# Another order of all engines in the middle of an attention and mixer kernel

## The chip, the core and the metric

The kernel runs on one core of a Trainium2 chip. The core has five engines that each run their own instructions in order and wait for one another through semaphores: PE (TensorE, matmuls; its weight loads are listed as PEld), DVE (VectorE), ACT (ScalarE), POOL (GpSimd) and SP (SyncE). DMAs are issued by POOL (loads here), SP (stores and transposes) and, at the end, ACT. The metric is the device time of one execution in microseconds (us). The profile is of one execution; its span runs from the first to the last instruction.

## What is computed

Block-causal attention over 8 batches, 8 heads, 576 positions and 64 channels a head, and then a token- and channel-mixing MLP on the result, in float32 at both ends:

```python
scores = (1 / sqrt(D)) * q @ k.T                # (8, 8, 576, 576), allowed where i // 64 >= j // 64
attn = softmax(scores); x = heads_to_channels(attn @ v)    # (8, 576, 512)
u = x + (relu(x.T @ w_tok1) @ w_tok2).T                    # 576 -> 256 -> 576 tokens
out = u + relu(u @ w_ch1) @ w_ch2                          # 512 -> 1536 -> 512 channels
```

## The kernel before

The kernel first records all its work as 1526 numbered pieces (`P.add`), each with the engines that may run it, the pieces it depends on and the PSUM banks that it takes and gives back. Nothing in it is looped on the chip. The order is a table, `ORDER`, of 1514 entries: `placed` walks through it, and each entry emits its piece at that point on the engine that it names. An entry such as `367Tdebf` is piece 367 on T (PE) in the PSUM banks d, e, b and f; A is ACT, D is DVE, P is POOL and S is SP; a to d are the `mm` banks, e to h the `late` banks. So the table sets three things: the order on each engine, the engine of a piece that two can run, and the bank. What it does not set are the waits: a piece waits for its inputs and for its bank wherever it stands.

The pieces of one batch, with their lines before the change (after it every line below the table is 3 higher):

- loads on POOL: q and k into `qk_sb` (L417, four a batch: two head groups of four heads), V into `vals` (L469, five a batch); they convert to bf16
- L440 on DVE: transposes of q and k inside 32 x 32 blocks, two for each load
- L562 on PE: score sets, three for each head group, in 32 rows of the array for each of four heads at a time
- L777 on ACT: exponentials from four PSUM banks into `e_sb`; L588 a copy of a part of it and L599 zeros for barred keys, on POOL or DVE
- L616 on PE: attention times V for one head (128 x 128 array), L669 the last 64 positions of four heads (64 columns); L636, L642 and L691, L697 on DVE: reciprocals and scaled results into `x_sb`, which give the bank back
- L814, L818 token matmuls up, L913, L944, L953 down, L928 their sum on DVE; L980 and L990 on SP: DMA transposes of it from batch 2 on
- L1041, L1114, L1238 channel matmuls up, the latter two with seven products for eight; L393, L395, L800, L802 evacuate banks on ACT or DVE, L1153, L1271 join on DVE
- L1354 sums for the channel matmuls down on DVE, L1372 those matmuls (256 columns each), L1396 folds their banks into `o_sb`, L1438 on SP stores it (L1483 for batch 0)

Attention of later batches stands between the channel matmuls of earlier ones, so PE has both kinds of work to hand. The first 44 us hold the loads of the weights and batch 0; attention ends with batch 7 at about 173 us; after that only token and channel matmuls are left.

Of the kernel before, what the change touches and what calls it, by code (L numbers as in the profile page):

```python
# [27 lines left out]
class Plan:  # L28
# [69 lines left out]
    9D 8D 14S 7D 0A 15A 11S 41Ta 19P 69Tb 17P 1D 52Tb 21P 31P 25P 51Tb 65Tb 23P 29P 12A 27P 3D 2D 16D 20D 18D 22D  # L98
    13D 26D 24D 105Ts 106A 98Ttbc 61Td 57Td 49Td 99A 100D 30D 63Td 118A 122Ts 70Td 123A 78Td 62Td 54Td 102Tt 103A
    45Td 28D 104D 35P 34P 50Td 33P 158Ts 159A 142Tt 143A 32P 74Td 181P 178P 101D 55Td 115Td 68Tb 125Ts 107Tb 184P  # L100
    108T 116D 117D 124D 183D 119A 162Tt 182D 160D 47Td 179D 40P 126A 138Ts 59Td 37P 42Td 109D 111Td 112T 120D 121D
    163A 66Tc 180D 145Tt 110D 39P 113D 144D 38P 36P 139A 135Tc 136D 114D 79P 127Ta 128T 131Tb 132T 133D 165Ts 80P
    140D 82P 161P 53Td 141D 146A 60Td 147Td 137D 129D 130D 166A 151Tc 152T 148T 134D 46Ta 44Ta 202Tabef 206A 204A
    205A 164D 185D 175Tg 153D 154D 155Th 149D 176D 177D 156D 157D 267Tc 268D 150D 203A 265Tg 167Th 208Tcbfe 266A
    187P 168T 81P 88P 87P 84P 83P 171Tg 89P 210A 269Td 209A 270A 90P 172T 211A 86P 85P 212A 343P 188D 273Tb 189D
    169D 170D 186D 277Th 173D 241Tdcaf 245A 174D 271Tg 10P 274D 244A 242A 275Tb 281Tf 278D 279Th 272D 285Tg 280A
    276D 195Tbdae 198A 197A 4D 282D 5D 286D 283Th 284D 310Tf 319Tg 287Th 288A 316Td 295Ta 317T 318D 320T 196A 243A
    322Th 323T 321A 199A 228Tdcbg 324A 200D 289Te 207D 290T 232A 230A 261D 296T 297A 6D 345D 311T 312D 231A 191P
    229A 192P 301Tc 193P 262D 346P 302T 235Taghb 239A 291A 236A 292Td 293T 233D 190P 194P 201P 344D 304Tb 294D 305T
    348D 234D 298Te 299T 347D 352P 216Td 219Ta 220D 237A 303A 217D 218D 213Tc 222Tg 306A 214D 223D 300A 238A 215D  # L110
    240D 225Th 226D 224D 367Tdebf 370A 227D 221D 313Tc 314T 369A 255Th 315D 373Tagbe 246Tc 368A 353D 371A 375A 354D
    307Td 376A 349P 247D 377A 256D 91P 248D 252Tf 308T 309A 257D 350D 351D 374A 258Tb 253D 360Tcegh 362A 361A 259D
    522P 364A 254D 334Td 249Te 519P 250D 251D 338Tf 393Thcae 260D 428Tb 395A 263D 264D 363A 520D 523D 396A 429D 397A
    394A 398D 426Tc 427A 92P 339T 372P 406Theag 409A 408A 93P 358P 432Tc 524D 433D 434Tb 435D 407A 340T 341D
    400Tceah 410A 430Tg 431D 436Tf 437D 335T 442Tg 404A 444Th 445D 403A 357P 521D 355P 402A 365P 359P 366P 401A
    446Tf 356P 378Tc 379D 387Te 388D 381Th 384Ta 405P 382D 389D 390Tb 447A 443A 380D 528P 391D 383D 392D 438Tg 385D
    399P 423Tc 424D 439A 536Thefb 537A 538A 539A 440Tg 540A 386D 336T 417Ta 425D 325Tc 549Tbfeh 94D 95D 441A 551A
    96D 450D 552A 531P 525P 97D 337D 329Tg 330T 454Tef 532P 553A 685P 451D 550A 533P 418D 535P 331T 411Tb 529D 332D
    527D 412D 413D 326T 420Tg 688P 421D 414Td 457A 460T 461A 469Thb 419D 422D 472A 455Ta 526D 691P 456A 415D 416D
    530D 470Tg 471A 541D 542P 327T 475T 476A 458Tg 452D 328D 453D 473Ta 543Tdhce 700P 459A 462T 687D 464T 474A 479T  # L120
    477T 546A 463D 547A 534P 544A 545A 690D 478D 569Tdgec 573A 572A 571A 701P 689D 480D 602Th 570A 603D 604Tc 605A
    576Thgea 578A 580A 548P 566Td 482T 577A 465D 466D 574D 467T 468A 694P 567D 568D 686D 612Td 613D 483D 582Thagc
    579A 585A 606Tf 857P 586A 557Te 610Td 581D 481D 584A 484Tbg 485Tc 611D 615S 583A 558D 487A 560Ta 559D 448Th 449A
    607D 608Td 486A 561D 609D 614S 490T 488Tf 491A 562D 554Th 692D 489A 563Te 564D 709Tabdc 711A 555D 556D 494T 342S
    565D 495D 492T 493D 575P 593Te 594D 590Th 591D 587Tb 588D 592D 710A 713A 712A 714P 497T 595D 498D 715Tdfca 333S
    589D 854P 599Th 596Te 597D 496A 697P 699P 695D 598D 716A 600D 719A 601D 870P 718A 696D 499D 500D 503Tgd 717A
    501D 504A 702Tebca 704A 616D 620Tfh 698P 623A 706A 863P 505T 693D 860P 705A 703A 707D 626T 627A 635Tab 507Tc
    638A 502D 641T 642A 506D 509T 508D 748Tgafe 751A 511T 617D 510D 512D 749A 859D 618D 858D 954P 752A 750A 513T
    735Tcaeg 736A 739A 708D 867P 770Tf 619D 514D 771A 855D 636Tc 737A 637D 856D 738A 740P 639Tg 515T 516D 742Tecaf
    862D 640A 645T 646D 745A 726Td 727D 643T 644D 865D 746A 720Ta 868P 768Tf 648T 723Tg 769D 721D 744A 728D 724D  # L130
    725D 624Tc 778Tf 722D 779D 774Td 729Tg 730D 731D 625A 628T 649A 776Ta 743A 747P 621Te 622A 777D 780Tg 781A 775D
    732Ta 783S 871Tdefb 874A 873A 875A 733D 629D 772Tg 647D 734D 741P 753Tc 773D 630T 650Tfa 653A 872A 762Tg 631D
    651Tb 652A 861D 759Te 754D 633T 755D 763D 764D 656T 657D 760D 761D 654Tb 634A 655A 878Tgchd 880A 879A 881A 864D
    765Tf 766D 660T 767D 756Te 757D 661D 658T 782S 819Tgf 758D 882A 822A 517S 804Thc 964P 807A 663T 659D 785D 786D
    789Tde 664A 792A 825T 632D 790Tb 787D 826A 662D 665D 951P 965P 960P 808Ta 809A 791A 866P 795T 796D 805Tg 810T
    806A 812T 813D 811A 793Tb 794A 814T 815D 917Thdga 799T 788D 876P 800D 797T 798D 918A 666D 919A 920A 921A 869P
    957P 820Th 817T 818A 823Tg 824A 802T 803A 967P 884Tabdc 888A 886A 821D 885A 887A 883P 667D 829T 827T 669Teh 670A
    830D 832T 956D 833A 828D 953D 904Tdabc 907A 877P 901Tg 668D 906A 902D 905A 955D 903D 908A 963P 952D 1051P 671T
    672D 911Tdabf 912A 914A 961D 895Tg 896D 897D 898Tc 899D 892Te 893D 915A 913A 900D 894D 937Td 938A 889Tg 981Tcafb
    985A 916D 909P 910P 890D 931Te 958D 932D 933D 984A 982A 673Td 891D 934Tg 983A 816A 959D 1057P 968Tecfb 970A 935D  # L140
    966P 936D 674D 972A 922Ta 923D 1054P 971A 924D 925Tg 926D 962D 1060P 927D 969A 675T 676D 928Ta 1066P 929D
    1008Tgfbc 1010A 677T 1011A 973P 1012A 1009A 930D 678D 975Tabfe 977A 979A 1053D 683S 679T 978A 1014Tebdg 1052D
    976A 680D 1015A 1017A 1055D 1016A 831D 939Tf 940D 1001Teacd 1018A 1002A 1004A 1062D 980P 974P 992Tb 986Tf 1003A
    1063P 995Tg 1061D 1056D 989Te 990D 1005A 993D 994D 1065P 991D 996D 681T 998Td 987D 1068Tebac 1071A 997D 1070A
    1072A 999D 988D 1069A 682D 943Tg 1000D 1036Tf 1058D 801D 1075Tdbha 1077A 1076A 944D 1006P 1079A 1059D 1037A
# [1441 lines left out]
```

## Time and profile before

| what | us |
|---|---|
| device time, median of 3 runs | 284.17 (284.06 to 284.25) |
| profiled execution, span of the core | 282.2 |
| what lies around the span, by the median | 2.0 |
| PE busy | 275.3 |
| DVE busy | 238.8 |
| ACT busy | 177.8 |
| POOL busy | 78.8 |
| last matmul ends, about | 278.7 |
| median landing of a 128 KB V load on POOL's queue | 5.9 |
| median landing of a 288 KB q load on POOL's queue | 6.1 |
| median landing of a 512 KB store on SP's queue | 3.0 |

Busy time on PE runs to the modelled end of each matmul, so back-to-back matmuls overlap in it and a busy PE may still be held back by a little less than one matmul's length; the step from start to start is the better measure. Sizes of the loads are those written, in bf16. A name such as `late<-vals,e_sb` says what an instruction writes and reads; PEclk, the granted clock, is full speed in all slices of the span.

### The profile page before, as it was taken

The page shows a single profiled execution, that of the slowest core. Times are in us where ns is not written, and L with a number is a line of the kernel's source. Part 1 is how long each engine was busy: PE and PEld are TensorE (multiplying, and loading weights), DVE is VectorE, ACT ScalarE, POOL GpSimd, SP SyncE. Part 2 cuts the span into 40 slices and gives each one's busy share as a digit, 9 for nine tenths or more (in the row PEclk, how much of TensorE's full clock was granted, in tenths as well). Part 3 has the DMA queues.
Part 4 walks back from the last instruction along what each step waited for, and adds up shares of the span by engine and source line. Part 5 has one row for each costly group of instructions (what it writes and reads, how often), then busy time and mean ns, then how long its engine had stood idle before and what let it go on. Part 6 is the DMA issues. An engine that isn't in the chain of part 4 may idle for free.

```text
span 282.2 us, 8544 instructions
## 1 busy us (share of the span) xinstructions
PE 275.3 (98%) x3580; PEld 193.2 (68%) x3580; DVE 238.8 (85%) x523; ACT 177.8 (63%) x326; POOL 78.8 (28%) x131
## 2 busy tenths in 40 slices
PE   7899999999999999999999999999999999999994
PEld 2457665475768877888776658744589664788884
DVE  4589598889889989999988879887797898898974
ACT  4788888775899774899997990326840858530000
POOL 8876726371613422092257210000000000000000
PEclk9999999999999999999999999999999999999999
DMA  8999999959958947699399465150127200020555
GB/s 160 167 153 194 191 200 203 162 63 170 95 88 229 150 67 56 151 104 127 46 118 161 31 141 120 42 114 19 37 49 210 80 0 0 3 75 14 212 126 174
DMA packets 64918, 31.75 MB, mean 112 GB/s; under 512 B 53104, under 2 KB 56176, under 8 KB 64880
## 3 DMA queue, kind: packets, MB, share of 16 engines
q0 software_dynamic: 45040, 17.64, 54.0%
q1 hardware_dynamic: 19408, 12.91, 16.7%
q10 hardware_dynamic: 432, 0.66, 0.7%
q8 instruction: 28, 0.46, 0.7%
q14 instruction: 10, 0.08, 0.1%
HBM read 35.85 MB, written 9.44 MB: 160 GB/s over the span
## 4 chain that ended last, share of the span: by engine, by line
PE 82%; DMA 10%; DVE 3%; ACT 2%; POOL 1%; issue 1%; DVEq 0%; POOLq 0%
PE mm L1372 13%; PE late L1372 11%; DMA qk_sb<-in_q_dram 7%; PE late L1114 7%; PE late L1238 6%; PE mm L1114 6%; PE mm L1238 6%; PE mm L562 4%; PE late L616 3%; DMA wc_sb<-in_moe_w_ch_dram 3%; PE late L562 3%; PE late L913 3%; PE mm L814 2%; PE mm L616 2%; PE late L814 2%; PE mm L913 2%
## 5 line engine op out<-in xcount | busy, mean ns | idle before, releaser
L777 ACT ACTIVATE e_sb<-mm 128x512 bf16<-128x512 f32 x94 | 53.5, 612 | 9.8 <-PE mm L562 4.2
L777 ACT ACTIVATE e_sb<-late 128x512 bf16<-128x512 f32 x74 | 43.0, 613 | 5.6 <-PE late L562 2.7
L440 DVE STREAM_TRANSPOSE qk_sb<-qk_sb 128x288 int32<-128x288 int32 (+2 forms) x57 | 38.3, 695 | 6.0 <-ACT qk_sb L393 1.9
L469 POOL DMA_DIRECT2D vals<-in_v_dram x45 | 37.1, 833 | 8.5 <-PE late L616 7.5
L1372 PEld LDWEIGHTS <-sums 128*128 128x128 bf16 x288 | 27.8, 98 | 4.2 <-issue 0.4
L1372 PEld LDWEIGHTS <-gT 128*128 128x128 bf16 x288 | 27.9, 98 | 3.7
L562 PEld LDWEIGHTS <-qk_sb 32*64 32x64 bf16 (+1 forms) x1024 | 16.9, 99 | 16.5 <-issue 9.6
L562 PE MATMUL mm<-qk_sb 32*64 32x320 bf16 (+6 forms) x534 | 27.7, 273 | 0.0
L616 PEld LDWEIGHTS <-e_sb 128*128 128x128 bf16 x640 | 23.9, 97 | 5.4 <-issue 0.9
L393 ACT COPY late<-mm 128x512 f32<-128x512 f32 (+1 forms) x14 | 8.0, 571 | 27.6 <-DVE o_sb L1396 14.5
L562 PE MATMUL late<-qk_sb 32*64 32x320 bf16 (+6 forms) x382 | 25.0, 277 | 0.3 <-DVE x_sb L642 0.3
L1114 PEld LDWEIGHTS <-ws_sb 128*128 128x128 bf16 x192 | 17.9, 98 | 4.2 <-issue 0.9
L599 POOL MEMSET e_sb<- 64x512 bf16 (+1 forms) x23 | 11.4, 511 | 31.7 <-ACT e_sb L777 28.4
L800 ACT ACTIVATE gT<-late 128x512 bf16<-128x512 f32 x20 | 12.2, 611 | 7.4 <-PE late L1114 4.9
L1114 PEld LDWEIGHTS <-wc_sb 128*128 128x128 bf16 x144 | 15.5, 113 | 1.8
L1238 PEld LDWEIGHTS <-ws_sb 128*128 128x128 bf16 x96 | 9.4, 98 | 9.8
L616 PE MATMUL late<-vals,e_sb 128*128 128x65 bf16 x360 | 15.8, 193 | 0.0
L642 DVE TENSOR_TENSOR x_sb<-late,rinv 128x256 bf16<-128x256 f32 x36 | 14.8, 418 | 0.7
L580 ACT ACTIVATE e_sb<-sc 128x1024 bf16<-128x1024 f32 x11 | 10.8, 1026 | 4.5 <-PE sc L562 4.5
L1372 PE MATMUL mm<-wd_sb,sums 128*128 128x256 bf16 x108 | 13.1, 273 | 0.0
L616 PE MATMUL mm<-vals,e_sb 128*128 128x65 bf16 x280 | 12.4, 193 | 0.0
L417 POOL DMA_DIRECT2D qk_sb<-in_k_dram x12 | 6.6, 551 | 20.7 <-ACT e_sb L777 7.1
(203 smaller groups left out, 649.4 us busy)
## 6 DMA issues: line engine op xcount, KB each, us to landing
out_dram<-o_sb SPq DMA_DIRECT2D x14, 512.0 KB, 3.0
vals<-in_v_dram POOLq DMA_DIRECT2D x28, 128.0 KB, 5.9
qk_sb<-in_k_dram POOLq DMA_DIRECT2D x12, 288.0 KB, 5.6
qk_sb<-in_q_dram POOLq DMA_DIRECT2D x12, 288.0 KB, 6.1
wc_sb<-in_moe_w_ch_dram POOLq DMA_DIRECT2D x8, 192.0 KB, 7.8
wc_sb<-in_moe_w_ch_dram POOLq DMA_DIRECT2D x3, 512.0 KB, 8.0
out_dram<-o_sb SPq DMA_DIRECT2D x4, 256.0 KB, 3.2
vals<-in_v_dram POOLq DMA_DIRECT2D x15, 64.0 KB, 5.4
```

The lines of the kernel that those rows point to most:

```text
L440: nc.vector.transpose(dst[:, 0:S, :] .rearrange("p s e -> p (s e)") .bitcast(I32) .rearrange("p (a k) -> p k a", k=NB)[:, k0:k1], raw2.bit ...
L469: nc.gpsimd.dma_start(out=t[128 - p : 128, J, hs, 0:64], in_=src)
L562: nc.tensor.matmul(out=home(n)[rows, c : c + w], lhsT=kT[i][r, 64 * j : 64 * j + keys, par], rhs=qT[i][r, 64 * q : 64 * q + w, par], start ...
L599: (nc.vector if o.engine == "DVE" else nc.gpsimd).memset(late_keys, 0.0)
L616: nc.tensor.matmul(out=u[:, I, 0:65], lhsT=e[:, h, c : c + 128], rhs=vt[:, J, head, 0:65], start=(J == 0), stop=(J == I),)
L642: nc.vector.tensor_tensor(out=xt[:, 0:4, 64 * head : 64 * head + 64], in0=u[:, :, 0:64], in1=ri[:, 0:4].to_broadcast([128, 4, 64]), op=MULT,)
L777: nc.scalar.activation(dst, bank_of(x), EXP, scale=scale)
L800: nc.scalar.activation(dst, src, RELU)
L913: nc.tensor.matmul(out=bank_of(bank), lhsT=w2_sb[:, t, 128 * si : 128 * si + 128], rhs=at[:, t, :], start=(t == 0), stop=(t == NDT - 1),)
L1114: nc.tensor.matmul(out=bank_of(bank)[:, 256 * o_ : 256 * o_ + 256], lhsT=x(o_, m), rhs=y[:, :, m, :], start=opens, stop=m == 1, skip_group ...
L1238: nc.tensor.matmul(out=bank_of(bank), lhsT=x(m), rhs=y[:, :, m, :], start=first and m == 0, stop=m == 1, skip_group_check=not first,)
L1372: nc.tensor.matmul(out=bank_of(bank)[:, 256 * i : 256 * i + 256], lhsT=x[:, kk, 128 * i : 128 * i + 128], rhs=y[:, kk], start=first and i ...
```

## The change

Only `ORDER` differs. All 1514 entries are there in both, the first 288 are the same, and the last 72 name the same pieces on the same engines, five of them with another bank letter. Between them the order of all engines is another one; 73 pieces change their engine (33 from ACT to DVE, 32 from DVE to ACT, 6 from DVE to POOL, 2 from POOL to DVE), and many banks change. The change is described as one that keeps loads away from stores. One line of each, the first that differs:

```diff
-    240D 225Th 226D 224D 367Tdebf 370A 227D 221D 313Tc 314T 369A 255Th 315D 373Tagbe 246Tc 368A 353D 371A 375A 354D
...
+    213Tc 222Tg 306A 214D 223D 300A 238A 215D 240D 225Th 226D 224D 367Tfbde 349P 91P 258Tc 369A 227D 92P 221D
```

The first place is on POOL, some 140 us into the run, where q and k of batch 7 are loaded. Before, its rows are these; the two q loads in one row are those of head groups 0 and 1 of batch 7, and the k loads ahead of them are the ones that go with them:

```order
L417 DMA qk_sb<-in_k_dram 128x1152
L588 COPY vals<-e_sb 128x256
L599 MEMSET e_sb 64x4x2x64
L417 DMA qk_sb<-in_k_dram 128x1152
L469 DMA vals<-in_v_dram 128x8x64
L417 DMA qk_sb<-in_q_dram 128x1152 x2
L469 DMA vals<-in_v_dram 128x8x64
L588 COPY vals<-e_sb 128x256
L599 MEMSET e_sb 64x4x2x64 x2
L469 DMA vals<-in_v_dram 128x8x64 x2
```

After, the same four loads, the q of head group 0 first, stand like this:

```order
L420 DMA qk_sb<-in_q_dram 128x1152
L591 COPY vals<-e_sb 128x256
L602 MEMSET e_sb 64x4x2x64
L420 DMA qk_sb<-in_k_dram 128x1152
L602 MEMSET e_sb 64x4x2x64
L420 DMA qk_sb<-in_q_dram 128x1152
L591 COPY vals<-e_sb 128x256
L602 MEMSET e_sb 64x4x2x64
L472 DMA vals<-in_v_dram 64x8x64
L420 DMA qk_sb<-in_k_dram 128x1152
L472 DMA vals<-in_v_dram 128x8x64 x2
```

The q load of head group 1 was issued last of the four, right behind the other q load; now it is issued third, with a copy, memsets and the k load of its group around it.

The second place is on DVE and belongs to the first: the transposes of those loads among the results of attention in batch 6 (L642). Before, the row of three transposes holds both of the q load of head group 1 and the second one of the other q load:

```order
L440 STREAM_TRANSPOSE qk_sb<-qk_sb 128x9x32
L1168 TENSOR_SCALAR gT<-gT 128x4x256
L802 TENSOR_SCALAR aT<-late 128x512
L440 STREAM_TRANSPOSE qk_sb<-qk_sb 128x9x32 x3
L636 RECIPROCAL rinv<-late 128x4
L636 RECIPROCAL rinv<-mm 128x4
L642 TENSOR_TENSOR x_sb<-mm,rinv 128x4x64
L642 TENSOR_TENSOR x_sb<-late,rinv 128x4x64
```

After, the last row is the first transpose of the q load of head group 1:

```order
L443 STREAM_TRANSPOSE qk_sb<-qk_sb 128x9x32
L639 RECIPROCAL rinv<-late 128x4
L639 RECIPROCAL rinv<-mm 128x4
L645 TENSOR_TENSOR x_sb<-mm,rinv 128x4x64
L645 TENSOR_TENSOR x_sb<-late,rinv 128x4x64
L639 RECIPROCAL rinv<-mm 128x4
L645 TENSOR_TENSOR x_sb<-mm,rinv 128x4x64
L645 TENSOR_TENSOR x_sb<-late,rinv 128x4x64
L443 STREAM_TRANSPOSE qk_sb<-qk_sb 128x9x32
```

Four results and their reciprocals have moved ahead of the transposes that read that q load.

The third place is on POOL again, where V of batch 4 is loaded. Before, the V row of two and the last V row are three of its five loads, with a V half of batch 5 between them:

```order
L599 MEMSET e_sb 64x4x2x64 x2
L417 DMA qk_sb<-in_k_dram 128x1152
L469 DMA vals<-in_v_dram 128x8x64 x2
L469 DMA vals<-in_v_dram 64x8x64
L469 DMA vals<-in_v_dram 128x8x64
L417 DMA qk_sb<-in_q_dram 128x1152
L417 DMA qk_sb<-in_k_dram 128x1152
```

After, the same row of two is the only one here of batch 4; the V rows on either side are of batch 5:

```order
L420 DMA qk_sb<-in_q_dram 128x1152 x2
L591 COPY vals<-e_sb 128x256
L602 MEMSET e_sb 64x4x2x64
L472 DMA vals<-in_v_dram 128x8x64
L420 DMA qk_sb<-in_k_dram 128x1152
L602 MEMSET e_sb 64x4x2x64
L472 DMA vals<-in_v_dram 128x8x64 x2
L472 DMA vals<-in_v_dram 64x8x64
L472 DMA vals<-in_v_dram 128x8x64
```

The two loads have moved behind two q loads, another V load, a k load and a copy with its memset; in the table they now stand directly ahead of the first L619 (L616 before) of batch 4. On SP the first store L1441 (L1438 before) has moved ahead of the second pair of transposes L983 (L980 before).

More of the change, by code (lines that the diff above doesn't have):

```diff
@@ new lines @@
+    543Tbghe 423Ta 547A 530D 546A 700P 687D 464T 690D 424D 698P 462T 463D 545A 544A 548P 473Te 474A 425D 694P
+    465D 438Th 439A 569Tacbg 479T 570A 554Th 573A 571A 477T 480D 478D 557Ta 558D 555D 556D 686D 691P 467T 572A
+    559D 482T 574D 468D 466A 576Tbceg 577A 483A 481D 602Th 578A 560Ta 561D 604Tb 579A 580A 562D 603A 605D
+    582Tacdf 583A 484Teg 487A 581D 585A 689D 608Tb 854P 609D 448Th 612Ta 613D 490T 575P 584A 563Tb 606Td 491A
+    701P 564D 610Ta 565D 488Tc 449A 586A 611D 607D 489A 566Th 567D 568D 709Tafbe 713A 485Td 693D 494T 486D 495D
@@ new lines @@
+    710A 492T 493D 712A 711A 599Ta 600D 715Tdheb 716A 497T 498A 614S 496D 596Tf 718A 601D 719A 717A 597D 598D
+    593Tc 587Td 588D 589D 503Tga 504A 594D 595D 615S 616D 590Tf 869P 702Tcdbe 706A 591D 592D 505T 620Tef 499D
+    704A 703A 623A 617D 635Tdh 636Tc 638A 637A 692D 506D 696D 507Tg 857P 770Tc 705A 641T 626T 500D 771A 333S
+    695D 501D 627D 342S 509T 508D 856D 642A 748Tdebc 511T 752A 502D 863P 621Tc 749A 707P 510D 751A 512D 750A
+    618D 639Td 640D 619D 513T 858D 514D 622A 735Tbceg 737A 736A 708P 738A 868P 859D 643T 644D 860P 645T 855D
@@ new lines @@
+    515T 516D 739A 646D 624Tc 647D 625A 742Tdebg 745A 714P 743A 697P 699P 723Ta 724D 870P 867P 628T 629D 740P
+    744A 630T 741P 631D 648T 746A 729Tb 720Tc 747P 725D 726Td 727D 730D 721D 731D 722D 768Te 649A 517S 756Ta
+    732Tc 728D 871Tbdgh 769A 772Te 873A 874A 872A 757D 758D 733D 734D 862D 773D 778Tc 779D 776Td 633T 650Tea
+    774Tc 777D 775D 759Tg 760D 761D 861D 753Tb 754D 762Td 783S 763D 954P 634A 653A 654Tf 656T 764D 655A 755D
+    632D 651Tc 657A 652A 660T 658T 659D 875A 876P 661D 878Tbced 877P 765Tg 964P 881A 879A 782S 882A 766D 780Tf
@@ new lines @@
+    890D 912A 898Tf 937Th 938A 903D 891D 892Tb 968Tacde 972A 969A 1051P 899D 916P 900D 893D 962D 970A 894D 1060P
+    675T 981Tebaf 971A 973P 958D 974P 934Tc 667D 668D 982A 967P 935D 931Td 932D 959D 928Th 922Te 929D 923D 924D
+    985A 936D 930D 673Tf 674D 984A 925Te 1057P 926D 927D 983A 1008Tbach 1010A 1012A 933D 1011A 677T 1009A
+    975Tdeah 965P 676D 977A 678D 831D 978A 979A 1063P 679T 1053D 1056D 1001Tbace 976A 1004A 680D 980D 1003A
+    1002A 939Tf 1005A 1052D 940D 1055D 1014Tadch 998Tb 1017A 992Tf 801A 1018A 995Te 999D 1000D 986Tc 989Tb 993D
@@ new lines @@
+    1058D 1006P 518S 681T 996D 1013P 990D 1015A 991D 997D 987D 988D 1007P 941Ta 994D 1016A 1068Tecdb 1031Th
+    1069A 1062D 1072A 1071A 945Tf 682D 942D 1064P 1065P 1025Te 1026D 1070A 946D 1027D 1036Tg 1037A 1075Tadbf
+    1028Tc 1076A 1061D 1059D 1032D 943Te 1033D 1022Tg 1023D 1077A 1078A 1034Ta 1079A 1035A 1066P 944D 1024D
+    1019Tb 1020D 1021D 1067P 1029D 1030D 816D 1108Tdehg 1112A 1110A 1109A 1046Tf 1047D 683S 1050S 1101Tabcg
+    1080D 1105A 1103A 1038Te 1039D 947Td 948D 950S 1044Tg 1073P 1111A 1268Tf 1113P 1104A 1102A 834D 1045D
@@ new lines @@
+    1149D 1151T 1296S 852S 1281S 1274Th 1212A 1414D 1207D 1145A 1147D 1417Tbe 1275D 1280S 1418Ta 1152A 1205A
+    1228D 1432Tdg 1290Th 1291D 1419A 1229D 1230D 1232Tcf 1433Ta 1415D 1420A 1233A 1231D 1423T 1234T 1235D 1225D
+    1238T 1239D 1236Tc 1242T 1297S 1237D 1243D 1240T 1299D 1300D 1421Th 1435A 1244T 1241D 1245D 1301D 1434A
+    1422A 1363Tac 1438T 1425T 1364Tf 1424A 1366A 1180A 1416D 1365A 1427T 1367Tb 1369T 1426D 1439A 1348Tfh 1428D
+    1430T 1368A 1351A 1371T 1165D 1302D 1431A 1372D 1349Td 1350A 1354T 1352Te 1373T 1374D 1436Td 1437D 1355A
```

125 lines of the change are left out of this document (49 added, 76 removed).

## The prediction

> **What bounds the kernel now.** I read the page first, then the busy times by stretch, then the list of who waited for whom on PE (TensorE), and at last the chain of waits. The page says that PE is hardly ever idle:
>
> ```profile
> span 282.2 us, 8544 instructions
> PE 275.3 (98%) x3580; PEld 193.2 (68%) x3580; DVE 238.8 (85%) x523; ACT 177.8 (63%) x326; POOL 78.8 (28%) x131
> ```
>
> A share over the whole span doesn't say where the rest lies. The view by stretch does (columns: length, then busy time and instructions of PE, PEld, DVE, ACT, POOL). I cut it at 44 us, where the first moved piece of PE's work starts, and at about 259 us, where the common end begins:
>
> ```profile
> 0.00:23.00 23.00, 20.14 (x290) 10.34 (x291) 14.46 (x50) 15.35 (x20) 18.94 (x36) 1.00 1.21 163
> 23.00:44.00 21.00, 20.78 (x352) 13.92 (x349) 17.34 (x45) 17.83 (x37) 10.85 (x19) 1.00 1.37 196
> 44.00:150.00 106.00, 106.00 (x1698) 76.64 (x1702) 96.90 (x224) 86.51 (x168) 42.03 (x65) 1.00 0.95 121
> 150.00:156.00 6.00, 5.69 (x160) 4.46 (x144) 5.46 (x17) 3.92 (x9) 4.64 (x7) 1.00 1.12 136
> 156.00:259.00 103.00, 103.00 (x926) 70.57 (x923) 88.46 (x160) 53.87 (x97) 2.36 (x5) 1.00 0.27 63
> ```
>
> PE is idle for 2.86 us before 23 us and 0.22 us up to 44 us; both lie in the part of the order that stays. In the 215 us whose order changes it is idle for 0.31 us, all of it between 150 and 156 us. The granted clock is 1.00 throughout. The waits of PE name the pieces:
>
> ```profile
> PE late L562 <- DVE x_sb L642: 0.3, 1, 0.3
> PE late L669 <- ACT e_sb L777: 0.2, 1, 0.2
> PE mm L814 <- DVE x_sb L642: 0.2, 1, 0.2
> ```
>
> The second is the 0.22 us before 44 us, the third belongs to the first 23 us. Only the first can go.
>
> Busy isn't yet full speed, since a matmul's record is longer than its step. So I look at the step, in the chain of waits, whose pieces run from one start to the next:
>
> ```profile
> 203.72 0.86 PE mm L1238 x4
> 255.67 2.62 PE mm L1372 x24
> ```
>
> A matmul of 512 columns takes 0.86 / 4 = 0.215 us and one of 256 columns 2.62 / 24 = 0.109 us: twice the columns, twice the time, so these pieces are bound by the columns streamed and nothing waits in them. The Trainium skill (TensorE: Matmul & The Clock Gate, Back-to-back issue gap) gives about 131 ns a matmul for a sustained stream at 512 columns, and N/2.4 + 2.5 ns for the isolated gap. By the first the long matmuls would have 39% of room and an order could win microseconds; the rows give 215 ns, which is the second, so the measurement decides and there is no such room.
>
> **The change, part by part.** Both programs hold the same matmuls (3580), in another sequence between 44 and about 259 us. So PE's own sum is the same, and only three things on it can change: its waits, its switches between array shapes, and nothing at the ends, which both orders share (the 2.0 us between the span of 282.2 and the median of 284.17 stays as well: I forecast changes against the profiled span and add them to the median).
>
> *The wait at 153.97 us.* The chain and PE's timeline show it:
>
> ```profile
> 143.94 7.26 DMA qk_sb<-in_q_dram
> ...
> 151.30 0.68 DVE qk_sb L440
> ...
> 152.40 0.70 DVE qk_sb L440
> ...
> 153.16 0.77 DVE x_sb L642 x2
> ...
> 153.97 0.30 PE late L562
> ```
>
> ```profile
> 153.46 0.20 PE L669 MATMUL mm<-vals 128*64 128x65 bf16 x2
> 153.97 0.30 PE L562 MATMUL late<-qk_sb 32*64 32x320 bf16 x1 [0.31 <-DVE x_sb L642]
> ```
>
> POOL issues a q load of batch 7 at 143.94 us, it lands 7.26 us later, DVE stands at its transposes until then, and only afterwards empties the PSUM banks of batch 6 (L642) that the scores of batch 7 need. The two short matmuls from 153.46 us step 65 columns each, some 0.06 us together, and a switch takes 0.10 (below), so L562 could have started at 153.62: the wait costs 0.35 us. In the new order DVE's rows have four L645 (L642 before) and their reciprocals ahead of the transpose pair of that load, and on POOL the load stands ahead of a V half, a k load and two V loads, where it followed a k, a V and the other q load. Both take this wait away. What is late next on PE there is unknown; the neighbouring stretches have no idle time, so I take minus 0.35 us.
>
> *Switches of shape.* L562 uses 32 rows of the array, L669, L944 and L953 use 64 columns, all else 128 by 128. PE's timeline around one set of scores shows the price:
>
> ```profile
> 97.09 1.47 PE L1372 MATMUL mm<-wd_sb,sums 128*128 128x256 bf16 x12
> 98.50 0.39 PE L562 MATMUL late<-qk_sb 32*128 32x512 bf16 x1
> ...
> 98.75 0.38 PE L562 MATMUL late<-qk_sb 32*128 32x512 bf16 x2
> 99.06 1.16 PE L1372 MATMUL mm<-wc_sb,sums 128*128 128x256 bf16 x9
> ```
>
> Twelve steps of 0.109 end at 98.40, and L562 starts at 98.50; its last 512 columns, from 98.75, end at 98.96, and L1372 starts at 99.06: 0.10 us a switch, each way. Counted over PE's whole order there are 121 switches before and 123 now, because sets of scores border less often on other work in small shapes: plus 2 x 0.10 = 0.20 us.
>
> *Work that changes engine.* 33 evacuations and casts go from ACT to DVE and 32 the other way, 6 small copies and memsets from DVE to POOL and 2 back. DVE (96.90 of 106 us busy in the long stretch) keeps about its load: one evacuation more, four small ones less. I take nothing; what covers it is that PE was never idle for DVE in that stretch, where the next matmuls stand ready while a bank is emptied. If the cover fails, one late evacuation costs at most its own 0.68 us:
>
> ```profile
> L1396 DVE TENSOR_TENSOR o_sb<-late,u_sb 128x512 f32<-128x512 f32 x12 | 8.2, 684 | 1.0 <-PE late L1372 0.6 <-issue 0.5
> ```
>
> *Stores and transposes on SP.* A store of batch 1 (L1441 now, L1438 before) moves ahead of the second pair of transposes, and single transposes change places later. No wait of PE's is put down to SP's queue: nothing, except what the store does to loads beside it, which is part of the first rival.
>
> *New waits.* Every reordered load or evacuation may come late; before, none did in 209 of 215 us. I take 0, with the worst case as a rival.
>
> Sum: -0.35 + 0.20 = -0.15, so 284.17 - 0.15 = **284.0 us**, no change by the 0.2% (0.57 us) that a measurement of this kernel can tell from none.
>
> **Rivals.**
>
> *Slower: V of batch 4 comes late.* These rows bear on it:
>
> ```profile
> 90.36 3.35 POOL L469 DMA_DIRECT2D vals<-in_v_dram  x4
> 106.81 0.46 PE L616 MATMUL mm<-vals,e_sb 128*128 128x65 bf16 x10
> DMA to landing us min/median/max: 3.2/5.7/9.2
> L469 POOL DMA_DIRECT2D vals<-in_v_dram x45 | 37.1, 833 | 8.5 <-PE late L616 7.5 <-issue 0.5
> L777 ACT ACTIVATE e_sb<-mm 128x512 bf16<-128x512 f32 x94 | 53.5, 612 | 9.8 <-PE mm L562 4.2 <-PE late L562 2.5 <-DVE qk_sb L440 1.6
> L599 POOL MEMSET e_sb<- 64x512 bf16 (+1 forms) x23 | 11.4, 511 | 31.7 <-ACT e_sb L777 28.4 <-DVE vals L588 1.5 <-PE late L562 1.1
> L393 ACT COPY late<-late 128x512 f32<-128x512 f32 x13 | 7.7, 591 | 1.5 <-PE late L1372 1.0 <-PE late L1114 0.3
> L588 POOL COPY vals<-e_sb 128x256 bf16<-128x256 bf16 x7 | 3.1, 446 | 8.8 <-ACT e_sb L777 6.3 <-issue 2.4
> L417 POOL DMA_DIRECT2D qk_sb<-in_k_dram x12 | 6.6, 551 | 20.7 <-ACT e_sb L777 7.1 <-DVE rinv L636 6.5 <-DVE qk_sb L440 6.3
> out_dram<-o_sb SPq DMA_DIRECT2D x14, 512.0 KB, 3.0
> ```
>
> Two V loads of batch 4 were issued in the group from 90.36 us, over 14 us before their reader (106.81). Now they stand on POOL behind a copy and a memset that wait for the exponentials of another score set of batch 4, and just ahead of their reader in the table. An estimate of their lead: from that set to the reader PE has 72 L1372 and 40 L1114 (112 x 0.109 = 12.2 us), one piece of token matmuls (1.1) and four sets of scores (0.6 each: 98.50 to 99.06 for the longest columns): 15.7 us. POOL's way to the second load: the scores 0.6, four exponentials 2.4, three L393 copies that ACT has between them 1.8, a copy and two memsets 1.5, the issue of two V loads and a k load 2.2: 8.5 us. That leaves 7.2 us, and less if the q load ahead of the copy still waits for DVE. At the median of 5.7 nothing waits; the point from which it decides is a landing over 7.2 us. The store that moved on SP, 3.0 us alone, may share the engines in those microseconds: 5.7 + 3.0 = 8.7, a wait of 1.5 us and a time of 284.0 + 1.5 = 285.5; at the longest landing, 9.2, it is 2.0 and 286.0. Against it: the median holds loads that stood in a row behind others, the least is 3.2.
>
> The Trainium skill (DMA: Bandwidth & Descriptors, Issuing engines are not separate DMA queues) says that all queues run on the same 16 engines and interleave, which speaks for this rival: a load beside a store waits whatever engine issued it. Its fit for such a load (Anatomy of one DMA, 2.0 us + bytes / 436e3) would give 2.6 us for 262 KB, an estimate by which the lead is ample; the median here is 5.7, and that counts.
>
> *Faster: holds too short to be shown go as well.* The profile names no idle time under 0.15 us. If three or four such holds in the long stretch went, 0.5 us more, the time would be 283.5. Against it: pieces of twelve L1372 in the chain are 1.31 us wherever I look, which is 12 x 0.109.
>
> *Nothing of it reaches PE.* If the wait only moves to another place, -0.35 falls away and the time is 284.4, still no change.
>
> **How the numbers follow.** The forecast and the third rival together 0.66, the slower one 0.20 (0.15 for V of batch 4, 0.05 for a late evacuation elsewhere), the faster one 0.14. These are the chances of same, slower and faster. The range leaves out the longest landings above and little below: 283.4 (0.1 under the faster rival) to 285.5 (the store beside the V loads).
>
> **What would show it.** Right: no PE wait for L645 near the first scores of batch 7, PE idle under 0.1 us from 44 to 259 us, steps of 0.215 and 0.109, and more than 215 us of that stretch busy. Wrong: a PE wait of L619 (L616 before) for a V load near 105 to 110 us, or for L443 transposes. A time below 283.6 would mean that PE held back in the long stretch without showing it.

## The result, and the profile after

The changed kernel took 285.83 us (median of 6 runs, 285.53 to 286.35), the kernel before 284.18 (6 runs, 283.64 to 285.08): a ratio of 1.0058, 95% interval 1.0043 to 1.0073, so 1.65 us slower. The prediction said 284.0, no change, with 285.5 as the upper end.

The page of the changed kernel (busy time, share of the span, instructions):

```profile
span 283.7 us, 8528 instructions
PE 274.5 (97%) x3558; PEld 193.4 (68%) x3580; DVE 241.1 (85%) x520; ACT 179.4 (63%) x325; POOL 80.5 (28%) x135
```

The span has grown by 1.5 us, as the time has, so the loss is in the trace. (22 of the 3580 matmul records are missing here. Most are of 512 columns; each of these leaves a gap of 0.215 us between two starts and up to 0.16 us of "idle" time, which mean nothing.) One run of experiment 5 and one of experiment 7 were slow, at a lower granted clock (0.982), and are left out of the medians and ranges given for them.

Its busy times by stretch, cut as before (columns as there; the end moved by 1.5 us):

```profile
44.00:150.00 106.00, 104.47 (x1645) 75.95 (x1659) 96.44 (x217) 83.36 (x161) 40.70 (x66) 1.00 0.97 125
150.00:156.00 6.00, 5.75 (x134) 4.14 (x144) 5.71 (x17) 5.65 (x11) 3.05 (x5) 1.00 0.47 103
156.00:260.50 104.50, 104.12 (x963) 71.48 (x963) 90.22 (x162) 56.81 (x99) 3.90 (x8) 1.00 0.32 60
```

PE was busy for all of the first stretch before; now 1.53 us are missing there, some tenths of it where a record is missing. The clock is 1.00 in both. The list of PE's waits says where most of it is:

```profile
PE late L1375 <- DVE o_sb L1399: 0.9, 1, 0.9
...
PE late L672 <- ACT e_sb L780: 0.2, 1, 0.2
PE mm L817 <- DVE x_sb L645: 0.2, 1, 0.2
```

The last two are the old ones of the first 44 us. The wait at L562 for x_sb, which the prediction took away, is gone. A new one, 0.9 us at L1375 for an evacuation by DVE, stands in its place. No load and no transpose is named. The chain of waits leads on from it (start, length, what; backwards from the last row):

```profile
88.49 4.89 DMA uT<-u_sb
...
93.47 0.42 DVE th_sb L1089
...
95.23 0.42 DVE th_sb L1089
95.65 0.63 DVE qk_sb L443
96.28 0.53 DVE o_sb L1399
96.81 0.04 issue
96.85 1.47 PE late L1375 x12
```

and the timeline of the same microseconds (in brackets the idle time ahead and what ended it) gives its links:

```profile
87.08 2.73 SPq L983 DMA_TRANSPOSE uT<-u_sb  x2
89.86 1.10 SPq L1486 DMA_DIRECT2D out_dram<-o_sb  x2
...
93.47 0.42 DVE L1089 TENSOR_TENSOR th_sb<-uT 128x512 bf16<-128x512 bf16 x1 [1.20 <-DMA uT<-u_sb]
...
95.37 0.60 PE L1117 MATMUL mm<-th_sb,ws_sb 128*128 128x256 bf16 x4
...
96.11 0.68 DVE L1399 TENSOR_TENSOR o_sb<-late,u_sb 128x512 f32<-128x512 f32 x1
...
96.85 1.47 PE L1375 MATMUL late<-wd_sb,sums 128*128 128x256 bf16 x12 [0.88 <-DVE o_sb L1399]
```

DVE stands still for 1.20 us at L1089, because the second of two transposes (issued 88.49) lands only at 93.37. Everything behind L1089 on DVE is late by as much, and with it the evacuation L1399 that frees a bank for PE. Four steps of 0.109 us from 95.37 end at 95.81, and PE's next start is at 96.85: 1.04 us too many. In the kernel before:

```profile
84.19 3.00 SPq L980 DMA_TRANSPOSE uT<-u_sb  x2
...
95.59 0.42 DVE L1086 TENSOR_TENSOR th_sb<-uT 128x512 bf16<-128x512 bf16 x1
```

Both transposes had landed by 89.1 us (3.2 us each) and DVE came to them at 95.59, 6.5 us later. In the new order the reader comes to its place at 93.47 - 1.20 = 92.27, 3.3 us earlier, and the later transpose is issued 2.6 us later. That leaves 3.8 us for a landing that took 3.2 before and 4.89 now.

### The profile page after: what moved, and what is told of

Its sections match the earlier page's. It is cut to its first block, busy times and chain, and to the rows that moved or that the text cites. A ratio compares the mean times of both kernels' runs of the same rounds, so it can differ in the third digit from the quotient of the medians.

```text
span 283.7 us, 8528 instructions
## 1 busy us (share of the span) xinstructions
PE 274.5 (97%) x3558; PEld 193.4 (68%) x3580; DVE 241.1 (85%) x520; ACT 179.4 (63%) x325; POOL 80.5 (28%) x135
## 4 chain that ended last, share of the span: by engine, by line
PE 78%; DVE 2%; DMA 2%; ACT 1%; issue 1%; SPq 0%; DVEq 0%; ACTq 0%
PE late L1375 16%; PE mm L1375 9%; PE late L1241 7%; PE late L1117 7%; PE mm L565 6%; PE mm L1241 6%; PE mm L1117 5%; PE mm L619 3%; PE mm L916 2%; PE late L619 2%; PE late L817 2%; PE mm L1466 2%; PE late L1466 2%; PE mm L817 2%; DMA uT<-u_sb 2%; PE late L916 2%
## 5 line engine op out<-in xcount | busy, mean ns | idle before, releaser
L780 ACT ACTIVATE e_sb<-mm 128x512 bf16<-128x512 f32 x99 | 55.4, 608 | 10.9 <-PE late L565 5.2
L780 ACT ACTIVATE e_sb<-late 128x512 bf16<-128x512 f32 x69 | 39.8, 610 | 8.6 <-PE late L565 3.7
L443 DVE STREAM_TRANSPOSE qk_sb<-qk_sb 128x288 int32<-128x288 int32 (+2 forms) x57 | 37.5, 693 | 5.1 <-ACT qk_sb L396 2.1
L1375 PEld LDWEIGHTS <-sums 128*128 128x128 bf16 x288 | 27.8, 98 | 5.8 <-issue 1.9
L1375 PEld LDWEIGHTS <-gT 128*128 128x128 bf16 x288 | 27.6, 98 | 4.2
L619 PEld LDWEIGHTS <-e_sb 128*128 128x128 bf16 x640 | 23.4, 97 | 3.5 <-issue 0.9
L565 PE MATMUL late<-qk_sb 32*128 32x448 bf16 (+6 forms) x362 | 25.6, 275 | 0.1
L1117 PEld LDWEIGHTS <-ws_sb 128*128 128x128 bf16 x192 | 18.1, 98 | 4.2 <-issue 0.9
L1117 PEld LDWEIGHTS <-wc_sb 128*128 128x128 bf16 x144 | 15.3, 114 | 3.2 <-issue 1.1
L645 DVE TENSOR_TENSOR x_sb<-mm,rinv 128x256 bf16<-128x256 f32 x40 | 16.2, 419 | 0.7
L396 ACT COPY late<-late 128x512 f32<-128x512 f32 x14 | 8.1, 579 | 13.7 <-PE late L1117 6.5
L619 PE MATMUL mm<-vals,e_sb 128*128 128x65 bf16 x400 | 16.4, 193 | 0.1
L396 ACT COPY mm<-late 128x512 f32<-128x512 f32 x21 | 11.9, 579 | 6.9 <-PE late L1241 4.8
L1375 PE MATMUL late<-wd_sb,sums 128*128 128x256 bf16 x120 | 14.8, 273 | 0.9 <-DVE o_sb L1399 0.9
L396 ACT COPY mm<-mm 128x512 f32<-128x512 f32 (+1 forms) x10 | 5.7, 565 | 15.2 <-PE mm L1375 14.5
L803 ACT ACTIVATE gT<-mm 128x512 bf16<-128x512 f32 x19 | 11.2, 609 | 5.9 <-PE mm L1241 4.2
```

The costliest lines, as they stand in the source:

```text
L396: nc.scalar.copy(dst, src)
L443: nc.vector.transpose(dst[:, 0:S, :] .rearrange("p s e -> p (s e)") .bitcast(I32) .rearrange("p (a k) -> p k a", k=NB)[:, k0:k1], raw2.bit ...
L565: nc.tensor.matmul(out=home(n)[rows, c : c + w], lhsT=kT[i][r, 64 * j : 64 * j + keys, par], rhs=qT[i][r, 64 * q : 64 * q + w, par], start ...
L619: nc.tensor.matmul(out=u[:, I, 0:65], lhsT=e[:, h, c : c + 128], rhs=vt[:, J, head, 0:65], start=(J == 0), stop=(J == I),)
L645: nc.vector.tensor_tensor(out=xt[:, 0:4, 64 * head : 64 * head + 64], in0=u[:, :, 0:64], in1=ri[:, 0:4].to_broadcast([128, 4, 64]), op=MULT,)
L780: nc.scalar.activation(dst, bank_of(x), EXP, scale=scale)
```

## The experiments

The theories: **A**, the stores issued right behind the transposes make the second one land late; **B**, its place does; **C**, the wait hides other holds of PE that would take its place; **D**, formed on the first four runs, a packet of TensorE's own code stands in its way. Edits of the table are shown by the entries around them; the number is that of the piece of work, the letter its engine.

**1. The two stores left out.**

```diff
...
                 def emit(o, oi=oi, i0=128 * (si - 1)):
-                    nc.sync.dma_start(
-                        out=out[0, i0 : i0 + 256, :].rearrange("(c p) d -> p c d", p=128), in_=o_sb[oi]
-                    )
+                    pass
```

> The changed kernel with the two stores of batch 0 (L1486, issued at 89.86 and 90.48 us behind the second pair of transposes) left out, so 512 rows of the output are not written; everything else stands where it stood. Theory A (the stores share the DMA engines with the second transpose, which lands 4.89 us after its issue instead of 3.2 to 3.4): it lands 3.2 to 3.5 us after its issue, DVE's 1.2 us at L1089 shrink to under 0.3, PE's 0.9 us at L1375 for o_sb go, 284.8 to 284.9 us. Theory B (its place alone makes it late: issued 4.3 us later than before and right behind the first one): it still takes about 4.9 us, the two waits stay, 285.8. Theory C (the wait at 97 us hides other holds of PE, which take its place): the two waits go and the time stays within 0.3 us of 285.8.

285.62 us (284.97 to 286.64); to before 1.0046 (1.0028 to 1.0063). The second transpose is issued at 88.18 and lands 4.87 us later, without any store beside it; DVE's and PE's waits stay. **A has fallen.** A wait that the changed kernel did not show came on top, at a V load of batch 4:

```profile
111.02 0.31 PE L619 MATMUL mm<-vals,e_sb 128*128 128x65 bf16 x5 [1.44 <-DMA vals<-in_v_dram]
```

With no store beside it one can see what the second transpose waits for. Of its 16 completions, 15 come 3.17 to 3.32 us after the issue and the last at 4.87 (in the changed kernel 15 by 3.34 and the last at 4.89). The view of the DMA engines for the 1.2 us in question (91.0 to 92.2 us; queue, packets, MB, share):

```profile
DMA packets 5, 0.02 MB, mean 14 GB/s; under 512 B 4, under 2 KB 4, under 8 KB 4
...
q8 instruction: 1, 0.02, 4.9%
q1 hardware_dynamic: 4, 0.00, 0.4%
```

and the trace's records of those packets (start in us, queue, bytes, ns):

```
91.01  q1    256   18
91.02  q1    256   18
91.04  q8  16384  941
91.96  q1      4   25
91.97  q1      4   21
```

The last two data packets of the transpose end at 91.04. Then a packet of 16 KB of the instruction queue takes 0.94 us, and only as it ends come the last two of the 32 words of 4 bytes by which the transpose reports; the other 30 were out by 2.68 us after the issue. (The records don't name a packet's DMA engine; that these are on the same one is read from the order of their times.) The page counts 28 such packets, in 7160 weight loads and matmuls: one for about every 256.

**2. The late evacuation put ahead on DVE.**

```diff
-505T 620Tef 499D 704A
+505T 620Tef 499D 506D 704A
...
-637A 692D 506D 696D 507Tg
+637A 692D 696D 507Tg
```

> The changed kernel with one entry of the table moved: the evacuation o_sb L1399 for which PE waits at 97 us (506) stands on DVE directly behind the first sums L1357 (499), ahead of th_sb L1089 and of a transpose L443. The stores and transposes stay, so DVE still waits about 1.2 us at L1089. Theories A and B (that wait reaches PE only through the evacuation queued behind it): the evacuation runs 0.8 us earlier, PE's wait falls from 0.9 to under 0.2 us, 284.9 to 285.0 us. Theory C: 285.6 to 285.9.

286.57 us (285.83 to 289.88); 1.0107 (1.0069 to 1.0144). The step did what A and B said: DVE waits 1.21 us as ever, L1399 follows the first sums at 94.83 instead of 96.11, and PE's wait at L1375 is no longer listed. Yet nothing is won, because PE now waits for V of batch 4:

```profile
108.84 0.31 PE L619 MATMUL mm<-vals,e_sb 128*128 128x65 bf16 x5 [0.48 <-DMA vals<-in_v_dram]
110.01 0.31 PE L619 MATMUL mm<-vals,e_sb 128*128 128x65 bf16 x5 [0.86 <-DMA vals<-in_v_dram]
```

This is the place of the prediction's slower rival, with 1.34 us where that had 1.5. In the profiled run of the changed kernel the wait at 97 us covers it: PE comes to the same matmuls 6.2 us after the issue of the V load instead of 5.4, and the load (issued 103.37, landed 109.74) is just in time. In experiment 1, with the same wait at 97 us, it was not. C in its general form (the time stays although the wait goes) came true, by a load. That POOL issues V so late is again DVE's doing, as POOL's rows of the changed kernel show:

```profile
99.09 0.55 POOL L420 DMA_DIRECT2D qk_sb<-in_q_dram  x1 [4.76 <-DVE qk_sb L443]
...
102.49 3.36 POOL L472 DMA_DIRECT2D vals<-in_v_dram  x4
```

The q load waits for a transpose L443 that stands on DVE behind L1089, and the V loads are issued behind the q load.

**3. The two transposes in the order of before.**

```diff
-497T 498A 614S 496D
+497T 498A 496D
...
-594D 595D 615S 616D
+594D 595D 615S 614S 616D
```

> The changed kernel with the two uT transposes of batch 3 in the order of before (615 ahead of 614 on SP); the stores follow them as in the changed kernel. The inputs of 615 are ready at 86.4 us, so it is issued there instead of at 88.5, and 614 about 1.3 us behind it. Theories A and B: the later of the two lands at about 91.3 to 92.2 us instead of 93.4, DVE waits under 0.2 us at L1089, PE's wait at L1375 goes, 284.8 us. Theory C: 285.6 to 285.9.

284.74 us (284.10 to 286.30, 12 runs); 1.0025 (1.0011 to 1.0040). The later transpose lands at 90.75, 3.16 us after its issue. On DVE nothing waits for it, and PE has neither wait:

```profile
91.90 0.41 DVE L1089 TENSOR_TENSOR th_sb<-uT 128x512 bf16<-128x512 bf16 x1
...
94.65 0.68 DVE L1399 TENSOR_TENSOR o_sb<-late,u_sb 128x512 f32<-128x512 f32 x1
...
95.46 1.47 PE L1375 MATMUL late<-wd_sb,sums 128*128 128x256 bf16 x12
```

The V load goes out at 101.90, 1.5 us earlier, and has landed at 107.64, ahead of PE. So about 1 of the 1.65 us hangs on this one change of places. B, "issued right behind the first one", is out as well: here the second is issued 1.41 us behind the first, as in the changed kernel, and lands in 3.16. But a code packet starts beside this transpose too, at 90.28 us, 2.69 us after its issue, and does not hold it: here all 32 words were out by 2.68. The same goes for experiments 6 and 10 (packets 2.55 and 2.56 us after the issue, landings 3.14 and 3.18). A landing of 4.89 would have come 0.6 us late for DVE here, by 87.59 + 4.89 against 91.90, so a part of this gain rests on some 0.2 us in the order of words and packet, and what sets that order was not tested.

**4. The two stores ahead of the transposes.**

```diff
-497T 498A 614S 496D
+497T 498A 333S 342S 614S 496D
...
-771A 333S 695D 501D 627D 342S 509T
+771A 695D 501D 627D 509T
```

> The changed kernel with the two stores of batch 0 ahead of both transposes on SP: they go out at about 68 to 70 us, beside the loads of POOL there. Theory A: the second transpose is alone again, lands 3.2 to 3.5 us after its issue, and the wait at L1375 goes: 284.8 us, unless the stores now delay a load that is waited for near 70 to 78 us (then a wait of DVE or PE for that load, up to 1.5 us). Theory B: transpose 4.9 us, 285.8.

286.33 us (285.31 to 286.98); 1.0073 (1.0054 to 1.0093). The second transpose takes 4.85 us with the stores gone from its neighbourhood, the wait at L1375 stays at 0.9, and 0.6 at a V load comes on top (and 0.5 for a load of weights at 26 us, which the changed kernel doesn't have). A has fallen a second time.

**5. The code moved.**

```diff
-            for _ in range(WARM):
-                nc.tensor.matmul(out=bank_of(bank), lhsT=zeros[:, 0:128], rhs=zeros, start=True, stop=True)
+            for _ in range(8 * WARM):
+                nc.tensor.matmul(out=bank_of(bank)[:, 0:64], lhsT=zeros[:, 0:128], rhs=zeros[:, 0:64], start=True, stop=True)
```

> The changed kernel with one edit far from the wait: the 11 matmuls of 512 columns that raise TensorE's clock at the start are written as 88 of 64 columns, 154 more PE instructions (weight loads and matmuls) and the same columns. Stores, transposes and order stay. In the trace PE's code arrives as 16 KB packets of one DMA engine about every 256 PE instructions, and one of them (91.35 us in the changed kernel, 91.04 without the stores) stands between the last data packet of the second transpose and its completion word. Theory D (this packet makes the transpose late): 154 instructions of about 0.032 us move it some 4.9 us ahead, the second transpose lands 3.2 to 3.5 us after its issue, DVE's 1.2 us at L1089 shrink to under 0.3, the wait at L1375 goes and, as with 615 first, the V loads come in time: 284.5 to 285.0 us. Theory B (its place behind the first transpose): still 4.9 us, 285.6 to 286.2.

286.06 us (284.29 to 287.70, 10 runs); 1.0065 (1.0034 to 1.0096). Half of D's forecast held. The packet starts at 87.50 instead of 91.35, before the transposes' data move; the second transpose, issued 88.96 behind the first and followed by both stores, lands 3.15 us later; and DVE does not wait:

```profile
92.45 0.41 DVE L1089 TENSOR_TENSOR th_sb<-uT 128x512 bf16<-128x512 bf16 x1
...
95.19 0.68 DVE L1399 TENSOR_TENSOR o_sb<-late,u_sb 128x512 f32<-128x512 f32 x1
```

So it was this packet that held the transpose up: of what stands near it only the time at which code arrives was changed. The same move put another packet (119.38) into the first transpose of the next pair, issued at 117.37: that one took 4.75 us where it took 3.23 in the changed kernel. The other half, the time, failed: another packet (106.67) now falls among the V loads, V takes 7.33 instead of 6.38 us, and PE waits there:

```profile
PE mm L619 <- DMA vals<-in_v_dram: 0.7, 2, 0.4
...
PE late L1117 <- DMA uT<-u_sb: 0.2, 1, 0.2
```

That the packet lengthens V's landing is argued from its place, not shown.

**6 and 7. V of batch 4 early, with each of the two cures.**

```diff
-616D 590Tf 869P 702Tcdbe
+616D 590Tf 697P 699P 869P 702Tcdbe
...
-714P 743A 697P 699P 723Ta
+714P 743A 723Ta
```

This edit is made beside that of experiment 3 (first text) and beside that of experiment 2 (second text).

> The kernel with 615 first, and besides the two V loads of batch 4 (697, 699) ahead of the V load 869 on POOL, so that they go out at about 82 to 83 us instead of 101 to 102. If the V loads still cost in part of the executions of the kernel with 615 first (its runs lie between 284.1 and 286.3): median 284.3 to 284.5, a narrower spread, no PE wait of L619 for V. If what is left there (284.74 against 284.05) is two more switches of shape and small holds of PE alone: 284.6 to 284.9.

> The changed kernel with the evacuation for which PE waits at 97 us put ahead on DVE (as in the second experiment) and the two V loads of batch 4 ahead on POOL. The transpose stays late and DVE still waits 1.2 us at L1089. If that wait of DVE reaches PE only by these two ways (the bank of L1375 and the V loads that POOL issues late): PE's waits of 0.9 at L1375 and 1.3 at L619 both go, 284.3 to 284.9 us. If DVE's lost 1.2 us come out elsewhere: 285.5 to 286 us, with a PE wait for DVE behind 100 us.

With 615 first: 284.51 us (284.11 to 285.02, 12 runs); 1.0017 (1.0004 to 1.0030), with a spread of 0.9 instead of 2.2 us; the median lies at the upper edge of the first forecast, and the spread is as it said. With the evacuation ahead: 284.59 (284.16 to 285.58, 11 runs); 1.0017 (0.9999 to 1.0035). V goes out at 82 to 83 us, and no PE wait behind 44 us is listed in either, though in the second DVE still loses 1.2 us at L1089. So what of that loss PE's list can show reaches PE by these two ways; some 0.2 us more may come in small holds (below).

**8. The prediction's first term by itself, in the kernel before.**

```diff
-1002A 1004A 1062D 980P
+1002A 1004A 980P
...
-995Tg 1061D 1056D
+995Tg 1056D
...
-999D 988D 1069A
+999D 988D 1062D 1061D 1069A
```

> The kernel before with one edit, which does the first term of the prediction alone: on DVE two transposes of batch 7 (1062, 1061), which the first scores of batch 7 don't need, stand behind the evacuations x_sb L642 of batch 6 instead of ahead of them. If the term stands by itself: PE's 0.31 us at L562 (153.97 us) go and nothing takes their place, 0.35 us less than before, about 283.7. If DVE has no room there (in 150 to 156 us it is busy for 5.5 of 6): a wait of 0.2 to 0.4 us comes back within 3 us, at the next scores or at L616, and the time is that of before, 284.0 to 284.1.

284.25 us (283.48 to 285.31, 12 runs), beside 284.29 for the kernel before; 1.0001 (0.9984 to 1.0019). The wait at the first scores of batch 7 is gone and comes back at the next ones, 3 us on:

```profile
157.02 0.37 PE L562 MATMUL mm<-qk_sb 32*128 32x448 bf16 x2 [0.32 <-DVE x_sb L697]
```

**9. The code moved in the kernel before** (edit of experiment 5).

> The kernel before with the edit of the fifth experiment alone (154 more PE instructions at the start, the same columns), so that the code packets come some 4.9 us earlier everywhere behind it. In the kernel before the transposes of batch 3 land over 6 us ahead of their reader and the V loads of batch 4 some 8 us. If the packets cost only where a transfer lands just in time: 283.8 to 284.4 us. If moved code costs by itself, or hits a transfer of this order too: 285 to 286, with a PE or DVE wait for a DMA that before doesn't have.

285.86 us (284.52 to 287.58, 12 runs); 1.0055 (1.0033 to 1.0076). A miss: I had expected this order to bear it. The transposes of batch 3 do (615 takes 4.95 us there and still lands 6.4 us ahead of its reader), but elsewhere PE waits (for V at 21 us, the others behind 44 us):

```profile
PE mm L562 <- issue: 0.9, 1, 0.9
PE mm L616 <- DMA vals<-in_v_dram: 0.8, 1, 0.8
PE late L562 <- issue: 0.4, 1, 0.4
```

The longest is in the middle of a set of scores, where nothing that the profile shows was waited for:

```profile
155.36 0.30 PE L562 MATMUL mm<-qk_sb 32*64 32x320 bf16 x2
156.53 0.33 PE L562 MATMUL mm<-qk_sb 32*64 32x320 bf16 x1 [0.87 <-issue]
```

A code packet ran there from 154.14 to 155.08, the first since 143.40. That PE had run out of code is one reading; but the packet's record ends 0.6 us before PE falls idle, and it was not tested.

**10 and 11. All three cures, and the code moved once more.** The first has the edits of experiments 2, 3 and 6, the second those of 3, 6 and 5.

> The changed kernel with all three edits: 615 first, the two V loads ahead of 869, the evacuation 506 ahead on DVE. If slack at these three places was all that it lacked against before, apart from two more switches (0.20 us) and small holds (0.1 to 0.2 in the trace of the kernel with 615 first): 284.2 to 284.5, and a narrower spread. Anything over 284.7 means that a wait which no trace shown so far has is left.

> The kernel with 615 first and early V loads, with the 154 more PE instructions of the fifth experiment. If slack ahead of the reader is what protects from a code packet: the spread of 284.3 to 290.5 of the fifth experiment shrinks and the median is 284.3 to 284.9. If the fifth was slow for another reason than the V loads (its trace has 0.36 us at L1117 for a transpose near 123 us too): 285.3 to 286.3 again.

All three: 284.40 us (283.87 to 285.72, 12 runs) beside 284.29 of before; 1.0012 (0.9995 to 1.0029), no longer to be told from the kernel before; the narrower spread that was expected did not come (1.9 us). With moved code: 284.95 (284.34 to 285.61, 12 runs); 1.0023 (1.0006 to 1.0039), a spread of 1.3 us where experiment 5 had 3.4, and no V wait; its median is at the upper end of the first forecast, and 0.3 us for a transpose at L1117 are left. No version was faster than the kernel before.

The readings side by side (us; the transposes of batch 3 by the one issued second, V by load 699; a wait that the list of the run doesn't name is a dash):

| kernel | transpose issued, landing | DVE at L1089 | PE at L1375 | V issued, landing | PE at L619 | time |
|---|---|---|---|---|---|---|
| before | 85.93, 3.17 | - | - | 91.24, 6.21 | - | 284.18 |
| changed | 88.49, 4.89 | 1.2 | 0.9 | 103.37, 6.38 | - | 285.83 |
| 1 no stores | 88.18, 4.87 | 1.2 | 0.9 | 103.05, 7.93 | 1.4 | 285.62 |
| 2 evacuation ahead | 88.09, 4.89 | 1.2 | - | 102.98, 6.99 | 1.3 | 286.57 |
| 3 615 first | 87.59, 3.16 | - | - | 101.90, 5.74 | - | 284.74 |
| 4 stores first | 89.11, 4.85 | 1.2 | 0.9 | 103.96, 7.12 | 0.6 | 286.33 |
| 5 code moved | 88.96, 3.15 | - | - | 102.45, 7.33 | 0.7 | 286.06 |
| 6 = 3, V early | 88.30, 3.14 | - | - | 82.75, 5.10 | - | 284.51 |
| 7 = 2, V early | 88.42, 4.88 | 1.2 | - | 82.28, 5.07 | - | 284.59 |
| 10 all three | 88.62, 3.18 | - | - | 83.09, 4.82 | - | 284.40 |

## Why the prediction was wrong

**The step that failed** is the one on stores and transposes on SP, priced at nothing. It said that single transposes change places and that no wait of PE's is put down to SP's queue, which was true and no answer. Their reader is DVE, and the time from the issue of the later one to its reader went from 9.7 to 3.8 us: the two tables show both moves (L1089 earlier on DVE, the pair turned round and later on SP), and the trace of before has the times. The prediction treated SP's moves only as neighbours of loads. With the 3.2 us that both took in the trace of before, 0.6 us would still have been left, and the new order would have got by; the 1.6 us that a code packet adds took that. I had not reckoned with such packets at all, though the page of before has them in its list of queues, and its trace has a transpose (issued at 113.10, a packet at 115.41) that landed only after 4.59 us: by that row the new order was already 0.8 us short.

**Work that changes engine: "at most its own 0.68 us".** The bound was wrong in kind. The evacuation L1399, which is on DVE in both kernels, cost PE 1.04 us, since it hands on what DVE had waited before it.

**The wait at 153.97 us, -0.35.** It went, and in the new order the stretch from 150 to 156 us is nearly full once the transposes are in time; the windows of the kernel with 615 first:

```profile
44.00:150.00 106.00, 105.98 (x1683) 76.50 (x1680) 97.47 (x219) 84.64 (x164) 40.44 (x65) 1.00 0.98 128
150.00:156.00 6.00, 5.94 (x148) 4.27 (x147) 5.85 (x17) 4.88 (x10) 4.49 (x7) 1.00 0.46 57
156.00:260.00 104.00, 104.00 (x916) 71.37 (x915) 89.61 (x160) 56.15 (x98) 2.46 (x6) 1.00 0.29 59
```

But the reason given, DVE's order at this place, is not enough by itself: experiment 8 changes just that, and the wait comes back 3 us later. What else of the new order carries it was not tried. The size was right: by the starts of the matmuls around it the wait cost 0.38 us.

**Switches of shape, +0.20.** Confirmed as far as the trace goes: 121 and 123, at 0.09 to 0.10 us each, in the traces with all matmuls recorded. The reason given is wrong: sets of scores border more often on work of 64 columns (17 times instead of 15), which stands in 19 separate groups instead of 17.

**The sum of -0.15 without waits.** From the same matmul (the 561st) to the last, PE took 237.84 us before, 239.32 in the changed kernel, and 238.04, 238.03 and 238.03 us in experiments 3, 6 and 10, where no wait behind 44 us is named beyond those of missing records. That is +0.20, not -0.15. (Experiment 7 has 238.26.) The rest, some 0.35 us, must then lie in holds under 0.15 us; two were found, 0.09 at a set of scores near 130 us and 0.12 at one near 150. The prediction had set these at zero on the word of a list that does not name them. The times agree: with all three cures 0.34 us more than before, with an interval from -0.14 to +0.82.

**The slower rival, V of batch 4.** Right in place and nearly in size, too low at 0.15. The lead, put at 7.2 us at most, was 6.2 in the changed kernel (issue 103.37, reader 109.58) and V took 5.7 to 7.9 in the runs that had it late. In experiment 2, where DVE still holds the q load up ("less if the q load ahead of the copy still waits for DVE") and PE is on time, it was 5.4. Whether the store "beside" has a part in the landing is open: in all these runs the store that moved, L1441, went out beside V, at 103.1 to 105.1 us, and no experiment took it away. In the changed kernel's profiled run V cost next to nothing, because PE was already late; that the rival's 285.5 lies near the measured 285.83 is therefore luck. Neither sign of being wrong that the prediction named stands in the changed kernel's list behind 44 us, and its sign of being right, "more than 215 us" busy, asked for more than the 215 us of the stretch.

So of the 1.5 us in the span 1.04 are one wait, started by a code packet and made possible by a lead cut from 9.7 to 3.8 us. The other 0.4 to 0.5 are switches and small holds, of which 0.2 are left once the wait is cured. V stands behind it as a second wait: it comes out when the first is taken away at PE alone, and in experiments 1 and 4 beside it.

## What to carry to other kernels

For every transfer that a reorder touches, write down its lead, from the issue to the reader on whichever engine that stands, before and after; a transfer that had 9.7 us and now has 3.8 is a risk, even if it took 3.2 in one trace. Set against it the longest landing of its kind in that trace (4.6 here), not the usual one. A wait of an in-order engine is paid by whatever is queued behind it, so an evacuation can be late by far more than its own length, and a load issued by another engine too. When the removal of a wait brings nothing, look for the next load on the same path before doubting the first reading: here two were stacked, and only the cures of both gave most of the time back.

## What the runs showed of the hardware

TensorE's code arrives during the run, 16 KB at a time (28 packets in this kernel, one for about 256 instructions), and each takes 0.88 to 2.4 us in the traces here. The transposes report in 16 parts and count as landed with the last: one such packet made a transpose of 3.2 us one of 4.9 (15 of 16 parts by 3.3), in the same way in all five traces that have the pair in the new order and the code in its old place. It did not do so in experiments 3, 6 and 10, where the packet started 2.55 to 2.69 us after the issue instead of 2.82 to 2.88. The start alone does not decide it: the packet 2.31 us behind the issue at 113.10 in the kernel before went with a landing of 4.59. The Trainium skill (Runtime: NRT & Kernel Launch, Instruction fetch mechanics) has the blocks of 16 KiB and 256 instructions, with which the count agrees (7160 / 28 = 256), and calls the cost of a block boundary "mostly hidden"; in the traces here it isn't hidden from the transfers beside it.

154 more instructions at the start of the program, with the same columns, cost the kernel before 1.6 us (experiment 9), and the changed one with two cures nothing that can be told (1.0023 in experiment 11 beside 1.0017 in 6). The place of the code packets against the work is thus part of what an order is worth, and with more instructions at the start (experiments 5, 9 and 11) the packets come at other times.
